# A gram of near tokens held by distance first and group second: one layout changed in a recurrent kernel on one core

## The chip, the cores and the metric

One core of a Trainium2 chip runs the whole program; the other cores are idle. The time is device microseconds from the start to the end of one execution, given as the median of several runs. The profile is that of one execution, and its own time is given beside it. The engines are called as in the profile: PE (TensorE, with PEld for its weight loads), DVE (VectorE), ACT (ScalarE), POOL (GpSimd) and SP (SyncE, which here only issues DMAs).

## What is computed

Two layers. The first is a recurrence over 768 tokens for 4 x 8 heads of 40 channels, in which each head keeps a 40 x 40 state:

```python
for t in range(S):
    y[:, :, t] = np.einsum('bhd,bhde->bhe', rt, state)
    Sa = np.einsum('bhde,bhe->bhd', state, at)
    state_decay = state * wt[:, :, None, :] - np.einsum('bhd,bhe->bhde', Sa, bt)
    state = state_decay + np.einsum('bhd,bhe->bhde', vt, kt)
```

The second takes each token's 320 numbers, normalises them by their root mean square, and puts them through a gated feed-forward layer of 1536 hidden units (`silu(x @ w_gate) * (x @ w_val) @ w_out`).

## The kernel before

The tokens are cut into 24 chunks of 32 (`C`). Inside a chunk the recurrence is replaced by a triangular system of scores between its tokens, so that all heads can be worked on with matmuls. Three functions write the pieces of work of a chunk. `front(c)` (L669) loads w, a, k, b and v, turns them, and makes the scores that only need the inputs; `inverse(c)` (L777), or `early_inverse(c)` (L795) for the first four chunks, inverts the triangle on DVE; `main(c)` (L827) joins it to the state and gives the chunk's outputs. After every second chunk `feed(g)` (L956) puts 64 tokens of each sequence through the feed-forward layer. That layer's matmuls (ps<-xg,wf and po<-wf,sg in the profile, L497) are the largest part of PE's time.

None of this is issued at once. Every operation becomes a `Piece`, and `Plan.issue` (L323) issues the pieces in the order of the list `ORDER` (L33 to L226), written out in the program: which piece comes next on any engine is fixed by that list, not by readiness. PSUM intermediates live in "rooms"; a room takes one of three pairs of PSUM banks, by the list `PAIRS` (L228), so a matmul that fills a pair waits until the last reader of that pair's earlier room is done. Because helpers such as `tt` (L457), `where` (L469), `copy` (L477) and `pe` (L502) record every operation, the profile's lines are those of the helpers: L455 is any DVE operation, L478 any ACT copy, L497 any matmul.

The change lies in `front(c)`, in the scores of near tokens. The 32 tokens of a chunk form 8 groups (g) of 4 tokens (j). Scores inside a group, at distances 1, 2 and 3, are made by one matmul per half and head, with 7 columns per group in the tile `A`: columns 0 to 2 for distance 1, columns 3 and 4 for distance 2 (multiplied by one step of decay), column 6 for distance 3 (by two), and column 5, which stays zero and whose results nobody reads. In order:

- L696: an ACT copy takes the a-part of the turned tile, tokens 1 to 3 of each group, into columns 0 to 2 of `A` (A<-ps in the profile). L697 puts tokens 0 straight into `Ab`, the operand of the next levels.
- L705, L706: two DVE products with the decay `w4` make columns 3 and 4, and column 6 (A<-A,T).
- L708: 32 matmuls per chunk write 56 columns each, 7 for each of 8 groups, into a room (ps<-A,K).
- L711 to L714: three DVE predicated copies, one for each distance, move these scores from PSUM into `LT`, where a mask `near` allows it (LT<-near,ps; they are called the near copies below). In `LT` and in `near` a row has 32 columns, group by group, 4 per group.
- L715 to L722: DVE products and an ACT copy make `K1`, the other operand of the next levels.
- L723 to L725: two DVE products put tokens 1 to 3 of each group into `Ab` (Ab<-A,T).
- L728 to L760: for distances 4, 8 and 16 the same again: a score matmul (ps<-Ab,K, L731), a predicated copy with the mask `msk` (LT<-msk,ps, L733), products and copies for the next level.

`main(c)` later reads scores in a like manner: L887 and L891 multiply them from PSUM by the mask `msi` into `As` (As<-ps,msi), at l=1 every second column, at l=2, 4 and 8 runs of l columns out of every 2l.

Of the kernel before, what the change touches and what calls it, by code (L numbers as in the profile page):

```python
# [9 lines left out]
U32 = mybir.dt.uint32  # L10
# [7 lines left out]
P = 128  # L18
# [361 lines left out]
def kernel(  # L380
# [42 lines left out]
    NI = 2 * N  # L423
# [14 lines left out]
    MUL, ADD, SUB = ALU.mult, ALU.add, ALU.subtract  # L438
    half = lambda i: slice(i * 64, (i + 1) * 64)
    part = lambda i: slice(i * 64, i * 64 + D)  # L440
# [12 lines left out]
    def dve(kind, fn, o, *args):  # L453
        m = lambda at: [at(x) if isinstance(x, bass.AP) else x for x in args]
        plan.add("DVE", kind, lambda at: fn(at(o), *m(at)), [o], aps(*args))  # L455

    def tt(o, a, b, op):  # L457
        dve("tt", nc.vector.tensor_tensor, o, a, b, op)
# [10 lines left out]
    def where(o, m, a):  # L469
        dve("where", nc.vector.copy_predicated, o, m, a)  # L470
# [6 lines left out]
    def copy(o, a):  # L477
        plan.add("ACT", "copy", lambda at: nc.scalar.copy(at(o), at(a)), [o], [a])  # L478
# [17 lines left out]
    def mm(o, lhsT, rhs, start=True, stop=True):  # L496
        return o, lhsT, rhs, lambda at: nc.tensor.matmul(at(o), lhsT, rhs, start=start, stop=stop, skip_group_check=True)  # L497
# [4 lines left out]
    def pe(kind, steps, more=[]):  # L502
        def issue(at):
            return [s[3](at) for s in steps]
        plan.add("PE", kind, issue, [s[0] for s in steps] + more, [x for s in steps for x in s[1:3]])
# [25 lines left out]
    for p0, kt, src in ((0, 0, 0), (0, 1, P), (0, 2, 2 * P), (64, 2, 2 * P)):  # L531
        m = min(P, DM - src)
# [7 lines left out]
    near = const.tile([P, 3, C], FP32, name="near")  # L540
# [39 lines left out]
    whole = lambda t: t  # L580
# [9 lines left out]
    Sd_ = Turns(2, [P, NI * D], "Sd", whole)  # L590
    T_ = Turns(3, [P, NI * 63], "T")
    K_ = Turns(2, [P, NI, 2, C], "K")
    A_ = Turns(1, [P, NI, 8, 7], "A", whole)

    Ab_ = Turns(2, [P, NI, C + D], "Ab")
    for t in Ab_.tiles:
# [38 lines left out]
    each = [(n, i, o) for n in range(N) for i in range(2) for o in range(2)]  # L635
# [33 lines left out]
    def front(c):  # L669
# [5 lines left out]
        for i in range(2):  # L675
# [6 lines left out]
            for x in range(2):  # L682
                at = i * 64 + x * C
# [5 lines left out]
        o = 0  # L689
        for l in LEVELS + (32,):  # L690
            Tl[l] = Tt[:, o:o + NI * C // l].rearrange("p (n t) -> p n t", n=NI)
            o += NI * C // l
        copy(by_i(Tl[1]), ps[:, :, :, 0])
        A, Ab = A_.next(), Ab_.next()
        a4 = ps[:, :, :, 1].rearrange("p n i t -> p (n i) t")
        copy(A[:, :, :, 0:3], a4.rearrange("p n (g j) -> p n g j", j=4)[:, :, :, 1:4])  # L696
        copy(Ab[:, :, 0:C].rearrange("p n (b h j) -> p n b h j", b=2, j=4)[:, :, :, :, 0], a4.rearrange("p n (h b j) -> p n b h j", b=2, j=4)[:, :, :, :, 0])  # L697
        K = K_.next()
        copy(K.rearrange("p (n i) x s -> p n i (x s)", n=N), turned(kb.rearrange("p n o e -> p n (o e)"), slot).rearrange("p n (i s) -> p n i s", i=2))
        LT = z["LT"] = LT_.next()  # L700
        z["KN"] = {1: flat(kb).rearrange("p a e -> p (a e)"), 2: KN_[2].next()}
        tt(z["KN"][2][:, 0:NI * D].rearrange("p (a e) -> p a e", e=D), flat(kb)[:, :, 0:D], wn, MUL)
        w4 = Tl[1].rearrange("p n (g j) -> p n g j", j=4)
        t2 = Tl[2].rearrange("p n (g x) -> p n g x", x=2)
        tt(A[:, :, :, 3:5], A[:, :, :, 1:3], w4[:, :, :, 1:3], MUL)  # L705
        tt(A[:, :, :, 6], A[:, :, :, 4], w4[:, :, :, 1], MUL)  # L706
        gr = plan.room().rearrange("p o (n t) -> p o n t", n=N)
        pe("gramk", [mm(gr[half(i), o, n, 0:56], K[part(o), 2 * n + i].rearrange("p x s -> p (x s)"),  # L708
                        A[part(o), 2 * n + i].rearrange("p g j -> p (g j)")) for n, i, o in each])
        g4 = gr.rearrange("p o n t -> p (o n) t")[:, :, 0:56].rearrange("p n (g j) -> p n g j", j=7)  # L710
        for dist, at in ((1, 0), (2, 3), (3, 6)):  # L711
            m = 4 - dist
            where(LT.rearrange("p n (g j) -> p n g j", j=4)[:, :, :, dist:], near[:, dist - 1:dist].rearrange(
                "p u (g j) -> p u g j", j=4)[:, :, :, dist:].bitcast(U32).to_broadcast((P, NI, 8, m)), g4[:, :, :, at:at + m])  # L714
        K1 = K_.next()  # L715
        lr = lambda t: t.rearrange("p n x (g h) -> p n x h g", h=2)
        tt(lr(K1)[:, :, :, 0], lr(K)[:, :, :, 0], lr(Tl[1][:, :, None])[:, :, :, 1].to_broadcast((P, NI, 2, 16)), MUL)
# [3 lines left out]
            k4 = K1[:, :, x].rearrange("p n (g j) -> p n g j", j=4)[:, :, :, 0:2]  # L721
            tt(k4, k4, t2[:, :, :, 1, None].to_broadcast((P, NI, 8, 2)), MUL)  # L722
        for x in range(2):  # L723
            tt(Ab[:, :, 16 * x:16 * x + 16].rearrange("p n (h j) -> p n h j", j=4)[:, :, :, 1:4], A[:, :, x::2, 0::3],
               w4[:, :, x::2, 0:1].to_broadcast((P, NI, 4, 3)), MUL)  # L725
        tt(Tl[4], t2[:, :, :, 0], t2[:, :, :, 1], MUL)
        K, A = K1, Ab
        for j, l in list(enumerate(LEVELS))[2:]:  # L728
            G = C // (2 * l)
            gr = plan.room().rearrange("p o (n t) -> p o n t", n=N)  # L730
# [7 lines left out]
            t = Tl[l].rearrange("p n (g x) -> p n g x", x=2)  # L738
# [21 lines left out]
            K, A = K1, A1  # L760
# [263 lines left out]
    for c in range(-2, NCH):  # L1024
        if c >= 0:
            main(c)
            if c % CG == CG - 1:
                feed(c // CG)
        if c + 2 < NCH:
            front(c + 2)  # L1030
            (early_inverse if c + 2 < EARLY else inverse)(c + 2)
# [34 lines left out]
```

## Time and profile before

| | |
|---|---|
| median of 3 runs | 1084.85 us (1081.85 to 1085.8) |
| the profiled execution, its own time | 1087.1 us |
| span of its profile, first to last instruction | 1085.0 us |
| mean granted TensorE clock in it | 0.979 |
| HBM traffic over the span | 111 GB/s |

A row of a group gives an operation with its output and inputs, their partitions x elements and how often it ran, then its total busy time, the mean duration in ns of one, the idle time of its engine just before it and what ended that idle time. A row of a timeline gives the start in us from the span's start, the time it took, and the instruction; in brackets stands how long the engine had idled and what released it. [...]

### The profile page before, as it was taken

To read this page: it belongs to the slowest core of one execution; us is meant where nothing else is said; L and a number is where in the kernel's file an instruction comes from. 1 tells how busy PE (TensorE), PEld (TensorE's weight loads), DVE (VectorE), ACT (ScalarE), POOL (GpSimd) and SP (SyncE) were. 2 spreads that over 40 slices of the span, in tenths; PEclk is the share of its full clock that TensorE was granted. 3 is DMA by queue.
4 is the path that set the end of the run, shared out by engine and by line. 5 is a ranking of instruction groups with operands and counts; after the bars stand their busy time and mean duration, and the time that the engine had idled before them with its cause. 6 is when DMAs were issued, how large, how long until landed. Compare 5 with 4: busy or idle time off the path is not lost. (4 is left out here: it accounts for less than half of the span.)

```text
span 1085.0 us, 53343 instructions
## 1 busy us (share of the span) xinstructions
PE 1008.5 (93%) x23406; PEld 828.7 (76%) x23406; DVE 833.1 (77%) x2860; ACT 461.7 (43%) x1043; POOL 309.0 (28%) x553
## 2 busy tenths in 40 slices
PE   7767899899999999999999999999889999999998
PEld 6656777777888787788788788787777787887776
DVE  7977778866868788798798798898778788796420
ACT  6845756643543334334344344434344244342211
POOL 9714404030532131341431321431332331200000
PEclk9978999999999899999999999999999999999999
DMA  9865338785363353555544534553544543623132
GB/s 177 191 164 120 67 93 214 227 166 137 86 139 84 81 130 72 120 107 101 116 92 108 120 92 107 121 111 92 114 89 95 128 109 59 143 70 89 58 103 67
DMA packets 166696, 123.67 MB, mean 114 GB/s; under 512 B 124864, under 2 KB 143232, under 8 KB 166464
## 3 DMA queue, kind: packets, MB, share of 16 engines
q1 hardware_dynamic: 148096, 97.30, 36.6%
q0 software_dynamic: 16192, 22.64, 12.0%
q8 instruction: 184, 3.01, 1.2%
q10 hardware_dynamic: 2176, 0.33, 0.3%
q14 instruction: 48, 0.39, 0.1%
HBM read 104.20 MB, written 15.99 MB: 111 GB/s over the span
## 5 line engine op out<-in xcount | busy, mean ns | idle before, releaser
L497 PE MATMUL ps<-xg,wf 128*128 128x256 f32 (+1 forms) x1728 | 353.9, 392 | 5.0 <-DVE tmp L455 1.4
L497 PEld LDWEIGHTS ps<-xg,wf 128*128 128x128 f32 (+1 forms) x1728 | 261.3, 189 | 60.5 <-issue 16.2
L497 PE MATMUL po<-wf,sg 128*128 128x320 f32 x576 | 181.7, 448 | 0.1
L455 DVE TENSOR_TENSOR tmp<-Yi,M 128x60 f32<-128x60 f32 (+24 forms) x620 | 129.4, 209 | 21.5 <-DMA M<-sB 8.8
L455 DVE TENSOR_TENSOR Yi<-Yi,tmp 128x60 f32<-128x60 f32 (+24 forms) x620 | 130.1, 210 | 12.4
L475 ACT ACTIVATE sg<-ps 128x256 f32<-128x256 f32 x144 | 52.2, 384 | 192.4 <-PE ps L497 192.2
L497 PEld LDWEIGHTS po<-wf,sg 128*128 128x128 f32 x576 | 103.7, 193 | 34.9 <-issue 3.1
L494 POOL DMA_DIRECT2D VU<-in_v_dram x92 | 53.7, 587 | 236.5 <-PE ps L497 154.2
L455 DVE TENSOR_TENSOR sg<-ps,sg 128x256 f32<-128x256 f32 x144 | 58.8, 419 | 59.0 <-ACT sg L475 52.5
L455 DVE TENSOR_TENSOR K<-K,T 128x512 f32<-128x512 f32 (+1 forms) x192 | 93.5, 496 | 8.4 <-PE ps L497 4.1
L497 PEld LDWEIGHTS ps<-Ab,K 40*64 40x64 f32 x4608 | 77.1, 137 | 29.2 <-issue 10.5
L478 ACT COPY KN<-ps 128x640 f32<-128x640 f32 x96 | 66.1, 690 | 75.7 <-PE ps L500 25.5
L497 PE MATMUL ps<-Ab,K 40*64 40x56 f32 x4608 | 86.5, 224 | 11.6 <-ACT K L478 4.7
L494 POOL DMA_DIRECT2D kbn<-in_b_dram x92 | 53.7, 587 | 142.6 <-PE ps L497 141.7
L455 DVE TENSOR_TENSOR As<-ps,msi 128x256 f32<-128x256 f32 (+1 forms) x186 | 79.2, 475 | 16.5 <-PE ps L497 15.4
L478 ACT COPY K<-K 128x256 f32<-128x256 f32 (+1 forms) x168 | 71.8, 443 | 39.1 <-DVE K L455 15.8
L497 PEld LDWEIGHTS ps<-As,KN 128*40 128x40 f32 x3072 | 65.5, 124 | 15.4 <-issue 10.0
L494 POOL DMA_DIRECT2D wn<-in_w_dram x92 | 51.7, 566 | 86.5 <-DVE KN L455 39.2
L497 PE MATMUL ps<-As,KN 128*40 128x32 f32 x3072 | 72.2, 204 | 3.9 <-issue 3.3
L494 POOL DMA_DIRECT2D kbn<-in_k_dram x92 | 53.6, 586 | 74.1 <-PE ps L497 73.3
L455 DVE TENSOR_TENSOR y<-y,ps 128x256 f32<-128x256 f32 x119 | 50.0, 420 | 18.5 <-PE ps L497 16.0
L455 DVE COPY_PREDICATED LT<-near,ps 128x384 f32<-128x384 uint32 (+2 forms) x72 | 52.3, 726 | 5.0 <-PE ps L497 3.9
(130 smaller groups left out, 1542.5 us busy)
## 6 DMA issues: line engine op xcount, KB each, us to landing
wf<-sW SPq DMA_DIRECT2D x104, 480.0 KB, 4.7
M<-sB SPq DMA_DIRECT2D x80, 128.0 KB, 3.3
sW<-ex SPq DMA_DIRECT2D x24, 240.0 KB, 4.4
rn<-in_r_dram SPq DMA_DIRECT2D x24, 160.0 KB, 4.3
out_dram<-ex SPq DMA_DIRECT2D x48, 80.0 KB, 3.2
kbn<-in_k_dram POOLq DMA_DIRECT2D x92, 40.0 KB, 3.3
kbn<-in_b_dram POOLq DMA_DIRECT2D x92, 40.0 KB, 3.6
wan<-in_a_dram POOLq DMA_DIRECT2D x46, 80.0 KB, 5.2
```

The lines of the kernel that those rows point to most:

```text
L455: plan.add("DVE", kind, lambda at: fn(at(o), *m(at)), [o], aps(*args))
L475: plan.add("ACT", "act", lambda at: nc.scalar.activation(at(o), at(a), f, **kw), [o] + aps(acc), [a])
L478: plan.add("ACT", "copy", lambda at: nc.scalar.copy(at(o), at(a)), [o], [a])
L494: plan.add(by, "dma", lambda at: queue.dma_start(out=o, in_=i), [o], [i])
L497: return o, lhsT, rhs, lambda at: nc.tensor.matmul(at(o), lhsT, rhs, start=start, stop=stop, skip_group_check=True)
```

## The change

`A` was held as 8 groups of 7 columns; it becomes 7 columns of 8 groups each. So the seven kinds of column come first and, within one kind, the eight groups lie side by side. The matmul at L708 still takes all 56 columns, and its 56 result columns in PSUM come in the new order. Each operation that writes or reads `A`, or reads those results, keeps its elements and walks them by column kind first and group second: the ACT copy at L696, the products at L705 and L706, the three near copies (whose walk through `LT` and `near` changes with it), and the two products into `Ab` at L723. Layouts of `LT`, `near`, `Ab` and `T` are as before, and so are the order of all instructions, their number, the PSUM pairs and all DMAs.

```diff
-    A_ = Turns(1, [P, NI, 8, 7], "A", whole)
+    A_ = Turns(1, [P, NI, 7, 8], "A", whole)
...
-        copy(A[:, :, :, 0:3], a4.rearrange("p n (g j) -> p n g j", j=4)[:, :, :, 1:4])
+        copy(A[:, :, 0:3], a4.rearrange("p n (g j) -> p n j g", j=4)[:, :, 1:4])
...
-        w4 = Tl[1].rearrange("p n (g j) -> p n g j", j=4)
         t2 = Tl[2].rearrange("p n (g x) -> p n g x", x=2)
-        tt(A[:, :, :, 3:5], A[:, :, :, 1:3], w4[:, :, :, 1:3], MUL)
-        tt(A[:, :, :, 6], A[:, :, :, 4], w4[:, :, :, 1], MUL)
+        w_j = Tl[1].rearrange("p n (g j) -> p n j g", j=4)
+        tt(A[:, :, 3:5], A[:, :, 1:3], w_j[:, :, 1:3], MUL)
+        tt(A[:, :, 6], A[:, :, 4], w_j[:, :, 1], MUL)
         gr = plan.room().rearrange("p o (n t) -> p o n t", n=N)
         pe("gramk", [mm(gr[half(i), o, n, 0:56], K[part(o), 2 * n + i].rearrange("p x s -> p (x s)"),
-                        A[part(o), 2 * n + i].rearrange("p g j -> p (g j)")) for n, i, o in each])
-        g4 = gr.rearrange("p o n t -> p (o n) t")[:, :, 0:56].rearrange("p n (g j) -> p n g j", j=7)
+                        A[part(o), 2 * n + i].rearrange("p j g -> p (j g)")) for n, i, o in each])
+        g4 = gr.rearrange("p o n t -> p (o n) t")[:, :, 0:56].rearrange("p n (j g) -> p n j g", g=8)
         for dist, at in ((1, 0), (2, 3), (3, 6)):
             m = 4 - dist
-            where(LT.rearrange("p n (g j) -> p n g j", j=4)[:, :, :, dist:], near[:, dist - 1:dist].rearrange(
-                "p u (g j) -> p u g j", j=4)[:, :, :, dist:].bitcast(U32).to_broadcast((P, NI, 8, m)), g4[:, :, :, at:at + m])
+            where(LT.rearrange("p n (g j) -> p n j g", j=4)[:, :, dist:], near[:, dist - 1:dist].rearrange(
+                "p u (g j) -> p u j g", j=4)[:, :, dist:].bitcast(U32).to_broadcast((P, NI, m, 8)), g4[:, :, at:at + m])
...
         for x in range(2):
-            tt(Ab[:, :, 16 * x:16 * x + 16].rearrange("p n (h j) -> p n h j", j=4)[:, :, :, 1:4], A[:, :, x::2, 0::3],
-               w4[:, :, x::2, 0:1].to_broadcast((P, NI, 4, 3)), MUL)
+            tt(Ab[:, :, 16 * x:16 * x + 16].rearrange("p n (h j) -> p n j h", j=4)[:, :, 1:4], A[:, :, 0::3, x::2],
+               w_j[:, :, 0:1, x::2].to_broadcast((P, NI, 3, 4)), MUL)
```

## The prediction

> **What bounds the kernel now.** First the page, for the span and the load of each engine, then its chain of work that ended last.
>
> ```profile
> span 1085.0 us, 53343 instructions
> PE 1008.5 (93%) x23406; PEld 828.7 (76%) x23406; DVE 833.1 (77%) x2860; ACT 461.7 (43%) x1043; POOL 309.0 (28%) x553
> PE 16%; issue 4%; DVE 3%; DMA 2%; POOL 1%; ACT 1%; SPq 0%; POOLq 0%; DVEq 0%; ACTq 0%
> ```
>
> TensorE (PE) is busy for 93% of the span and leads the chain, so PE sets the time; every engine's order is written out by hand and stays. The change alters no matmul: the one that makes the near scores still has 56 columns, only named in another order. It alters VectorE (DVE) and ScalarE (ACT) instructions, and it costs or gains only what they make PE wait. Next I read the groups by line with the shapes kept apart, for the instructions that are rewritten and for plain neighbours to measure them against (busy us, mean ns of one, idle before).
>
> ```profile
> L455 DVE TENSOR_TENSOR As<-ps,msi 128x256 f32<-128x256 f32 x144 | 54.2, 415 | 14.0 <-PE ps L497 12.9 <-ACT As L481 0.8
> L455 DVE COPY_PREDICATED LT<-msk,ps 128x256 f32<-128x256 uint32 x72 | 31.2, 433 | 15.3 <-PE ps L497 8.2 <-ACT KN L478 6.3
> L455 DVE TENSOR_TENSOR As<-ps,msi 128x512 f32<-128x512 f32 x42 | 28.4, 680 | 2.5 <-PE ps L497 2.5
> L455 DVE TENSOR_TENSOR Ab<-A,T 128x192 f32<-128x192 f32 x48 | 21.0, 444 | 0.2
> L455 DVE COPY_PREDICATED LT<-near,ps 128x128 f32<-128x128 uint32 x24 | 17.5, 728 | 0.4
> L455 DVE COPY_PREDICATED LT<-near,ps 128x256 f32<-128x256 uint32 x24 | 17.4, 725 | 0.3
> L455 DVE COPY_PREDICATED LT<-near,ps 128x384 f32<-128x384 uint32 x24 | 17.4, 724 | 4.3 <-PE ps L497 3.9 <-DMA LT<-sY 0.2
> L455 DVE TENSOR_TENSOR A<-A,T 128x256 f32<-128x256 f32 x24 | 10.9, 456 | 4.4 <-ACT T L478 3.3 <-ACT A L478 1.0
> L455 DVE TENSOR_TENSOR T<-T 128x256 f32<-128x256 f32 x24 | 10.1, 420 | 2.7 <-ACT T L478 2.5
> L455 DVE TENSOR_TENSOR A<-A,T 128x128 f32<-128x128 f32 x24 | 9.6, 400 | 0.2
> L455 DVE TENSOR_TENSOR T<-T 128x128 f32<-128x128 f32 x24 | 6.9, 286 | 0.1
> L455 DVE TENSOR_TENSOR tmp<-Yi,M 128x70 f32<-128x70 f32 x20 | 4.8, 238 | 0.4
> ```
>
> The two T<-T rows give the plain price: (420 - 286) / 128 = 1.05 ns an element and 420 - 256 * 1.05 = 152 ns fixed. The three predicated copies into LT (the near copies, 24 chunks each) stand far above it, and they take **the same 725 ns for 384, 256 and 128 elements**. What the three share is 128 runs, of 3, 2 and 1 elements: (726 - 152) / 128 = 4.5 ns a run.
>
> **Which side of the copy costs this.** This decides the sign. A run lies in PSUM 7 columns (28 bytes) from the next, in LT and in the mask 4 words (16 bytes). Three rows speak for LT and the mask.
> First, PSUM jumps are cheap elsewhere: among the 415 ns multiplies from sc are those with l=2 (pairs, a jump of 4 columns after each, 128 of them), and those with l=1 read every second column within the 680 ns row; both are at the plain price (152 + 512 * 1.05 = 690).
> Second, the msk copies write 64 pieces of 16 bytes whatever l is. At 4.5 ns a piece that is 152 + 288 = 440, at the plain price 421; they show 433, while multiplies with the same PSUM reads show 415.
> Third, the timeline of one chunk:
>
> ```profile
> 827.42 0.73 DVE L455 COPY_PREDICATED LT<-near,ps 128x384 f32<-128x384 uint32 x1
> 828.02 0.40 DVE L455 TENSOR_TENSOR K<-K,T 128x256 f32<-128x256 f32 x1
> 828.34 0.72 DVE L455 COPY_PREDICATED LT<-near,ps 128x256 f32<-128x256 uint32 x1
> ...
> 828.69 1.24 PE L497 MATMUL po<-wf,sg 128*128 128x320 f32 x4
> ...
> 829.24 0.71 DVE L455 COPY_PREDICATED LT<-near,ps 128x128 f32<-128x128 uint32 x1
> 829.58 0.43 DVE L455 TENSOR_TENSOR tmp<-Yi,M 128x70 f32<-128x70 f32 x1
> ...
> 830.00 1.16 PE L497 MATMUL ps<-Ab,K 40*64 40x56 f32 x64
> ```
>
> The copy of 128 elements lets the next instruction begin after 0.34 us, and that one takes 0.43 us in place of 0.24 (its row above): the reads were done early and results queued up. I read this as a slow write; a slow PSUM read with many requests in flight would look alike, so it is no proof.
> [...]
>
> **The change part by part** (per chunk; 24 chunks).
> *Near copies.* The element order becomes distance, then group, so each element lies 16 bytes from the one before in LT and in the mask, and PSUM is read in runs of 8. The copy at distance 3 has the same LT and mask walk as before; at 728 ns for 128 single visits it is the nearest row for the others. I take its 4.5 ns for each element: 384 give 152 + 384 * 4.5 = 1880, 256 give 1304, 128 stay at 728; together 3912 against 724 + 725 + 728 = 2177, **+1.73 us**. Lower end: the plain price, 555 + 421 + 286 = 1262, -0.92 us.
> *Products into A and Ab on DVE.* The nearest row for words read one by one is the 400 ns product (steps of 28, 28 and 16 bytes): (400 - 152) / 128 = 1.94 ns an element. The 256-element product keeps a single stepped operand, T: at 1.94 it is 649, at 1.05 421 (456 now); the 128-element one 286 to 400; the two into Ab write and read T in single words, 524 at 1.94 (444 now), 354 at 1.05. Taking 1.94: 193 + 0 + 2 * 80 = **+0.35 us**; lower end 2 * (354 - 444) + (421 - 456) + (286 - 400) = -0.33.
> *ACT copy into A.* Its writes become contiguous, its PSUM reads single columns.
>
> ```profile
> L478 ACT COPY T<-ps 128x512 f32<-128x512 f32 x24 | 14.2, 591 | 15.1 <-PE ps L500 13.7 <-DVE Yi L455 1.3
> L478 ACT COPY A<-ps 128x384 f32<-128x384 f32 x24 | 13.9, 579 | 3.9 <-PE ps L500 3.9
> L478 ACT COPY Ab<-ps 128x128 f32<-128x128 f32 x24 | 9.5, 397 | 4.2 <-PE ps L500 4.2
> L478 ACT COPY M<-ps 128x128 f32<-128x128 f32 x8 | 2.2, 277 | 5.0 <-PE ps L497 5.0
> ```
>
> Contiguous: (591 - 277) / 384 = 0.82 ns an element, 172 fixed, so 384 give 487 (-0.09 us). If single columns cost what the Ab row shows, (397 - 172) / 128 = 1.76, it is 848 (+0.27). I take nothing: ACT is busy 43% of the span; without that cover it is at most 24 * 0.27 = 6.5 us.
> *Moves.* None: the same instructions in the same order on every queue, no DMA touched, no wait added.
>
> **What reaches PE.** Behind a near copy stand, in DVE's queue, the K products that the next score matmul (ps<-Ab,K) needs, and in most chunks that matmul writes the pair of PSUM banks that the near copies read. So the lag from the end of the third copy to that matmul is the room for delay. Above it is 830.00 - 829.95 = 0.05 us. Some others:
>
> ```profile
> 370.53 0.72 DVE L455 COPY_PREDICATED LT<-near,ps 128x128 f32<-128x128 uint32 x1
> ...
> 373.82 1.16 PE L497 MATMUL ps<-Ab,K 40*64 40x56 f32 x64
> ...
> 656.60 0.73 DVE L455 COPY_PREDICATED LT<-near,ps 128x128 f32<-128x128 uint32 x1
> ...
> 657.71 0.51 PE L497 MATMUL ps<-Ab,K 40*64 40x56 f32 x19
> ...
> 786.46 2.25 DVE L455 COPY_PREDICATED LT<-near,ps 128x384 f32<-128x384 uint32 x3 [0.61 <-PE ps L497]
> ...
> 788.77 0.45 PE L497 MATMUL ps<-Ab,K 40*64 40x56 f32 x15 [0.38 <-DVE LT L455]
> ```
>
> At 788.77 PE already waits for the copy. Read so for all 24 chunks: nine lags of 0.05 to 0.38 (sum 1.7), four of 0.7 to 1.1 (sum 3.7), one of 1.5, three of 2 to 2.9, and in seven the matmul starts before the third copy ends. The +0.35 us comes earlier, and DVE can lose it while it waits. In the windows from the first A product to the first near copy:
>
> ```profile
> core 0: us, PE busy (x) PEld busy (x) DVE busy (x) ACT busy (x) POOL busy (x), PEclk, DMA share, GB/s
> ...
> 650.40:654.90 4.50, 4.50 (x87) 3.62 (x84) 4.46 (x12) 1.73 (x3) 3.06 (x6) 1.00 0.80 196
> 814.30:827.40 13.10, 12.05 (x184) 9.78 (x184) 10.65 (x38) 4.49 (x10) 2.89 (x6) 1.00 0.78 156
> ```
>
> The first has no idle time to give, the second 2.4 us. Ten chunks have under 0.3 us, so I carry half: the delay at the lag is 1.73 + 0.17 = 1.9 us. PE then loses 9 * 1.9 - 1.7 = 15.4, 4 * 1.9 - 3.7 = 3.9, 0.4, and nothing in three chunks; for the seven I take half the delay, 6.7, between nothing and 13.3 there. **Sum 26.4 us.** It holds if PE's order cannot make up what it loses, which 93% busy suggests. The profiled execution took 1087.1 us (span 1085.0), 0.2% above the median of 1084.85, so 1113 in a profile and **1111 us** beside that median. Ends: everything through, 24 * (1.73 + 0.35) = 50 us, 1135; and below, the rivals.
>
> **Rivals.**
> *A, PSUM's spread columns are the cost (ends on the other side).* Place: the read of ps in the near copies; it decides if the distance-3 copy, whose LT and mask walk is untouched, falls below 700 ns. For it: all three copies jump 28 bytes, which no other DVE row does. Against it: the l=2 multiplies. Then the copies fall to the plain price, -0.92, with +0.35 for the products -0.57 us a chunk; the same share as above (26.4 of 50, half) gives -7 us, 1078; without the product cost -12, 1073. [...]
> *B, single words cost what a plain product pays.* At 1.94 ns the copies take 897 + 649 + 400 = 1946, -0.23, the products +0.35: +0.12 us a chunk, 1.5 us in all, 1086. For it: the 400 ns row, with no queue behind it. Against it: the distance-3 copy at 4.5. [...]
> *C, the slow copies are covered.* DVE idles 1085 - 833 = 252 us; if only the chunks with no lag pass half of it on, 9 * 0.9 = 8 us, 1093. Against it: the wait at 788.77.
>
> **How the numbers follow.** Forecast 0.62; A 0.14; B 0.17; C 0.07. Half a per cent, 5.4 us, is what a measurement here can tell from no change, so same means 1079.4 to 1090.3. A gives faster 0.14; B splits, 0.11 same and 0.06 slower; with the forecast and C slower is 0.75. The range leaves A out and reaches from B to the upper end with a little room: 1084 to 1138.
>
> **What would show it.** [...] The products into A and Ab at about 650, 400 and 524. More waits of PE for LT, and ps<-Ab,K right behind the third copy in most chunks. I am wrong if the copies are slow and the span is not, or if the span grows with the copies at their old price.

## The result and the profile after

The changed kernel took **1127.16 us** (median of 6 runs, 1123.27 to 1136.88), the kernel before 1083.12 us in the same comparison (6 runs, 1075.49 to 1085.8): a ratio of **1.0424, 95% interval 1.037 to 1.0479**, some 46 us slower. The forecast was 1111 us. The profiled execution of the changed kernel took 1123.27 us itself, its span 36.2 us more than that of before. The spans differ by less than the medians because the profiled execution of before (1087.1 us) lies 4.0 us above its median and that of the changed kernel 3.9 us below.

The page of the changed kernel, in the lines that answer to those of before; PEclk is the granted TensorE clock in tenths over 40 equal slices.

```profile
span 1121.2 us, 53343 instructions
PE 1030.3 (92%) x23406; PEld 844.4 (75%) x23406; DVE 879.1 (78%) x2860; ACT 460.6 (41%) x1043; POOL 310.3 (28%) x553
PEclk8776899999999999999999899999999999999999
PE 15%; DVE 5%; issue 4%; DMA 2%; POOL 1%; ACT 1%; POOLq 0%; DVEq 0%; ACTq 0%
```

DVE is busy for 46.0 us more, and its share of the chain goes from 3% to 5%. But PE too is busy for 21.8 us more (1030.3 against 1008.5) with the same 23406 matmuls. The mean granted clock is 0.956, against 0.979; by slices it was, before:

```profile
PEclk9978999999999899999999999999999999999999
```

PE's idle time (span less busy) grows by only 14.4 us, from 76.5 to 90.9.

The groups of the changed kernel by line, shapes apart:

```profile
L455 DVE COPY_PREDICATED LT<-near,ps 128x384 f32<-128x384 uint32 x24 | 44.8, 1868 | 3.3 <-PE ps L497 3.2
L455 DVE COPY_PREDICATED LT<-near,ps 128x256 f32<-128x256 uint32 x24 | 30.9, 1288 | 0.3
L455 DVE TENSOR_TENSOR Ab<-A,T 128x192 f32<-128x192 f32 x48 | 24.6, 521 | 0.2
L455 DVE COPY_PREDICATED LT<-near,ps 128x128 f32<-128x128 uint32 x24 | 17.4, 724 | 0.4
L455 DVE TENSOR_TENSOR A<-A,T 128x256 f32<-128x256 f32 x24 | 14.9, 622 | 2.5 <-ACT T L478 2.5
L478 ACT COPY A<-ps 128x384 f32<-128x384 f32 x24 | 12.1, 503 | 3.1 <-PE ps L500 3.1
L455 DVE TENSOR_TENSOR A<-A,T 128x128 f32<-128x128 f32 x24 | 9.4, 391 | 0.2
L497 PE MATMUL ps<-Ab,K 40*64 40x56 f32 x4608 | 88.3, 228 | 28.9 <-DVE K L455 7.5 <-DVE LT L455 6.2 <-ACT K L478 5.7
```

The near copies take 1868, 1288 and 724 ns. That is 152 + 4.5 ns for each element, as forecast, and 1.70 us more a chunk. The products take 622, 391 and twice 521 ns, 0.31 us more; the ACT copy takes 503 ns, 76 less than before.

The last row holds 28.9 us of idle time ahead of the score matmul; the same row of before, which follows, held 11.6.

```profile
L497 PE MATMUL ps<-Ab,K 40*64 40x56 f32 x4608 | 86.5, 224 | 11.6 <-ACT K L478 4.7 <-issue 3.5 <-ACT ex L475 0.9
```

**Where PE waits.** Two places of the prediction, found again in the timeline of the changed kernel: the copies that began at 786.46 (PE idle 0.38 us at 788.77), and those that began at 827.42 (PE did not wait at 830.00).

```profile
814.85 3.95 DVE L455 COPY_PREDICATED LT<-near,ps 128x384 f32<-128x384 uint32 x3 [0.61 <-PE ps L497]
...
818.85 1.16 PE L497 MATMUL ps<-Ab,K 40*64 40x56 f32 x64 [2.08 <-DVE LT L455]
...
856.31 1.89 DVE L455 COPY_PREDICATED LT<-near,ps 128x384 f32<-128x384 uint32 x1
858.37 1.28 DVE L455 COPY_PREDICATED LT<-near,ps 128x256 f32<-128x256 uint32 x1
859.83 0.70 DVE L455 COPY_PREDICATED LT<-near,ps 128x128 f32<-128x128 uint32 x1
860.58 1.15 PE L497 MATMUL ps<-Ab,K 40*64 40x56 f32 x64 [1.76 <-DVE tmp L455]
```

In the first chunk the three copies take 3.95 us in place of 2.25, and PE's idle time goes from 0.38 to 2.08: 1.70 us longer on DVE, 1.70 us lost on PE. In the second PE waits 1.76 us where it did not wait. The releaser named there is tmp, the DVE instruction issued behind the third copy; the matmul still starts 0.05 us after that copy ends, as before.

Not every wait stands at that matmul. At 303.93 in the changed kernel the wait comes ahead of a matmul in between, at a place where before had none:

```profile
299.91 3.96 DVE L455 COPY_PREDICATED LT<-near,ps 128x384 f32<-128x384 uint32 x3
...
303.93 0.84 PE L497 MATMUL ps<-VU,KN 64*40 64x40 f32 x63 [1.32 <-DVE LT L455]
```

So I measure the stretch from the start of a chunk's first near copy to its score matmul. Summed over the 24 chunks it grows from 76.8 to 102.9 us (+26.1), and PE's idle time inside it from 2.5 to 29.9 us (**+27.4**). The forecast had 26.4 there.

**Two terms that the sum did not have.** The span is 36.2 us longer. The waits behind the near copies are 27.4 of it; PE's idle time everywhere else is 13.0 us less (14.4 - 27.4); and PE's own busy time is 21.8 us more. The last goes with the granted clock. In the records it is either full or half (1.00 or 0.50 of full speed). By the mean clocks, PE had half the clock for (1 - 0.979) * 2 * 1085.0 = 46 us before and (1 - 0.956) * 2 * 1121.2 = 99 us after; 53 us more at half clock and 21.8 us more busy is 0.41 us for each. The two spans, cut at the same point of the work (where chunk 5's near copies begin), first before, then after:

```profile
core 0: us, PE busy (x) PEld busy (x) DVE busy (x) ACT busy (x) POOL busy (x), PEclk, DMA share, GB/s
0.00:190.20 190.20, 151.35 (x4118) 132.10 (x4119) 150.75 (x467) 118.90 (x251) 87.88 (x176) 0.92 0.68 147
190.20:1085.00 894.80, 857.16 (x19290) 696.58 (x19289) 682.34 (x2394) 342.79 (x792) 221.16 (x377) 0.99 0.46 107
```

```profile
0.00:198.40 198.40, 163.90 (x4116) 143.49 (x4117) 160.06 (x468) 119.83 (x252) 88.83 (x176) 0.83 0.66 142
198.40:1121.20 922.80, 866.43 (x19292) 700.94 (x19291) 719.07 (x2394) 340.80 (x792) 221.51 (x377) 0.98 0.45 103
```

In the first fifth, where PE already had the most gaps, the clock falls from 0.92 to 0.83, and PE is busy 12.5 us longer for the same matmuls; its idle time even shrinks, from 38.9 to 34.5. So busier PE is more than the whole loss of 8.2 us there, although PE waits 4.7 us more in the stretches above: its other idle time fell by 9.0. Behind it the 28.0 us are 9.3 of busier PE and 18.7 of idle time.

**What halves the clock.** One and the same wait, in chunk 8, is in the changed kernel and in an experiment below (e2, in which only the copies changed). The timeline of the changed kernel, then of the experiment:

```profile
339.52 1.34 PE L497 MATMUL ps<-Ab,K 40*64 40x56 f32 x64 [1.72 <-DVE K L455]
340.80 3.43 PE L497 MATMUL ps<-xg,wf 128*128 128x256 f32 x8
```

```profile
337.37 1.16 PE L497 MATMUL ps<-Ab,K 40*64 40x56 f32 x64 [1.71 <-DVE K L455]
338.45 1.99 PE L497 MATMUL ps<-xg,wf 128*128 128x256 f32 x8
```

After equal waits, the same eight matmuls take 3.43 us in the one and 1.99 us in the other. In both traces every change of the clock lies on a grid of 3.41 us. Cut on that grid, the same two places read (changed kernel first; the number after POOL's is the clock):

```profile
333.49:336.90 3.41, 3.41 (x18) 2.74 (x18) 3.32 (x6) 1.01 (x1) 0.00 (x0) 1.00 0.69 107
336.90:340.32 3.42, 1.70 (x60) 1.25 (x62) 2.96 (x9) 1.70 (x5) 0.00 (x0) 1.00 0.33 126
340.32:343.73 3.41, 3.41 (x33) 2.77 (x24) 2.61 (x11) 0.41 (x1) 0.00 (x0) 0.50 0.00 0
```

```profile
333.33:336.74 3.41, 2.33 (x14) 1.45 (x12) 2.94 (x7) 1.88 (x4) 0.00 (x0) 1.00 0.90 212
336.74:340.15 3.41, 2.78 (x72) 2.49 (x73) 3.31 (x13) 1.15 (x3) 0.00 (x0) 1.00 0.04 16
340.15:343.56 3.41, 3.41 (x135) 2.70 (x134) 2.23 (x7) 1.64 (x5) 0.00 (x0) 1.00 0.02 5
```

In the changed kernel the wait falls whole into one window: PE is busy for 1.70 of 3.42 us in it, and the next window has half the clock. In the experiment the same wait lies across the border of two windows, PE is busy for 2.33 and 2.78 us in them, and the clock stays full. Counted on this grid over the 13 traces of this case, without the start and the end of each (up to the first fall of the clock, and the window before the last), of the windows with full clock all 47 with PE busy for under 40% were followed by half clock, 26 of 36 with 40 to 50%, 42 of 79 with 50 to 60%, 25 of 133 with 60 to 70%, and 4 of 3527 with 70% or more. So a wait of 1.7 us costs PE itself, or itself and, in these rows, (3.43 - 1.99) + (1.34 - 1.16) = 1.6 us more, by where it lies on the grid.

### The profile page after: what moved, and what is told of

Its sections match the earlier page's. It is cut to its first block, busy times and chain, and to the rows that moved or that the text cites. A ratio compares the mean times of both kernels' runs of the same rounds, so it can differ in the third digit from the quotient of the medians.

```text
span 1121.2 us, 53343 instructions
## 1 busy us (share of the span) xinstructions
PE 1030.3 (92%) x23406; PEld 844.4 (75%) x23406; DVE 879.1 (78%) x2860; ACT 460.6 (41%) x1043; POOL 310.3 (28%) x553
## 5 line engine op out<-in xcount | busy, mean ns | idle before, releaser
L497 PE MATMUL ps<-xg,wf 128*128 128x256 f32 (+1 forms) x1728 | 363.4, 398 | 7.3 <-DVE sg L455 2.6
L497 PEld LDWEIGHTS ps<-xg,wf 128*128 128x128 f32 (+1 forms) x1728 | 267.7, 193 | 65.5 <-issue 16.6
L497 PE MATMUL po<-wf,sg 128*128 128x320 f32 x576 | 182.8, 450 | 0.9 <-DVE sg L455 0.9
L497 PEld LDWEIGHTS po<-wf,sg 128*128 128x128 f32 x576 | 104.3, 194 | 36.2 <-issue 3.7
L497 PEld LDWEIGHTS ps<-Ab,K 40*64 40x64 f32 x4608 | 79.2, 141 | 47.6 <-issue 15.4
L497 PE MATMUL ps<-Ab,K 40*64 40x56 f32 x4608 | 88.3, 228 | 28.9 <-DVE K L455 7.5
L455 DVE COPY_PREDICATED LT<-near,ps 128x384 f32<-128x384 uint32 (+2 forms) x72 | 93.1, 1293 | 3.9 <-PE ps L497 3.2
L497 PEld LDWEIGHTS ps<-As,KN 128*40 128x40 f32 x3072 | 66.3, 125 | 12.3 <-issue 7.2
L497 PE MATMUL ps<-As,KN 128*40 128x32 f32 x3072 | 72.2, 206 | 1.5 <-issue 1.0
L455 DVE TENSOR_TENSOR y<-y,ps 128x256 f32<-128x256 f32 x119 | 50.0, 420 | 14.3 <-PE ps L497 11.6
```

## The experiments

Ratios are to the kernel before, run on the same chip. A time without an interval is one execution; the kernel before, beside those, took 1095.59 us, which lies above all its other runs, so that only durations are read from them.

**Which part costs: the copies or the rest.** e1_groups_first keeps the new layout and all else, but the near copies walk group by group again, through `LT`, `near` and `g4` as in the lines removed by the change:

```diff
-        g4 = ....rearrange("p n (j g) -> p n j g", g=8)
+        g4 = ....rearrange("p n (j g) -> p n g j", g=8)
...
-            where(LT.rearrange("p n (g j) -> p n j g", j=4)[:, :, dist:], near...
+            where(LT.rearrange("p n (g j) -> p n g j", j=4)[:, :, :, dist:], near...
```

> The changed kernel, with the three near copies alone walking group first again: LT and the mask in runs of 3, 2 and 1 as before the change, PSUM in single columns 8 apart. Price per 16-byte piece of LT and mask (theory L): the copies are back at 725 ns each, whatever PSUM's order. If PSUM's order has a price of its own (rival P): the copies of 384 and 256 elements take over 800. The products into A and Ab stay at 622, 391 and 521, the ACT copy at 503, so DVE has about 24 * 0.31 = 7.5 us more than before the change. Time: if nearly all DVE delay reaches PE (theory T) +6 us on the kernel before, about 1089; if half reaches it and the rest of the loss came from the granted clock (rival C) +4, about 1087.

Measured: 1075.61 us against 1077.14, ratio 0.9996, 0.9965 to 1.0027; neither of the two expected losses, 4 and 6 us, came. The groups of this kernel:

```profile
L455 DVE COPY_PREDICATED LT<-near,ps 128x128 f32<-128x128 uint32 x24 | 17.5, 729 | 0.4
L455 DVE COPY_PREDICATED LT<-near,ps 128x384 f32<-128x384 uint32 x24 | 17.4, 726 | 3.2 <-PE ps L497 3.0
L455 DVE COPY_PREDICATED LT<-near,ps 128x256 f32<-128x256 uint32 x24 | 17.4, 726 | 0.3
```

PSUM is read here in single columns, 8 apart, and the copies still take 726 ns: the order of the PSUM columns costs and gains nothing. Rival A is out. The slower products (624, 394 and 523 ns) are in this kernel as well, and cost nothing that can be measured.

e2_copies_only is its mirror: the old layout, and only the copies walk by distance first.

```diff
-        g4 = ....rearrange("p n (g j) -> p n g j", j=7)
+        g4 = ....rearrange("p n (g j) -> p n j g", j=7)
...
-            where(LT.rearrange("p n (g j) -> p n g j", j=4)[:, :, :, dist:], near...
+            where(LT.rearrange("p n (g j) -> p n j g", j=4)[:, :, dist:], near...
```

> The kernel before, with the three near copies alone walking distance first: A and the products as before, LT and the mask word by word, PSUM in single columns 7 apart. Theory L: 1868, 1288 and 725 ns as in the changed kernel, though PSUM's columns are not neighbours. Rival P: more than that, above 2000 for 384 elements, since PSUM now jumps too. DVE has 24 * 1.71 = 41 us more than before. Time: theory T (0.8 to 0.9 of it reaches the end) +33 to +37, 1116 to 1120; rival C, the forecast's share of one half and little from the rest: +22, 1105, with the granted clock near that of the kernel before.

Measured: 1115.91 us, ratio 1.0382, 1.0329 to 1.0435. The copies take 1866, 1288 and 724 ns. Nearly the whole loss comes with the copies' walk alone, and it is more than either expectation (22, or 33 to 37 us): some 41. Between this kernel and e1, on one chip, the profiled spans differ by 38.9 us: 18.2 of busier PE (1027.2 against 1009.0) and 20.7 of idle time, with clocks of 0.958 and 0.977. In the stretches from the first near copy to the score matmul PE idles 24.3 us more (27.9 against 3.6).

**Which side of the copy.** Three kernels take its operands apart. e3_mask_dense stores the mask in the order in which the copies read it:

```diff
-        ts(near[:, dist], bits, float(dist + 1), None, ALU.is_equal)
-        tt(near[:, dist], near[:, dist], same, MUL)
+        nd = near[:, dist].rearrange("p (j g) -> p g j", g=8)
+        ts(nd, bits.rearrange("p (g j) -> p g j", j=4), float(dist + 1), None, ALU.is_equal)
+        tt(nd, nd, same.rearrange("p (g j) -> p g j", j=4), MUL)
...
-                "p u (g j) -> p u j g", j=4)[:, :, dist:]...
+                "p u (j g) -> p u j g", g=8)[:, :, dist:]...
```

> The changed kernel with the mask near stored in the order in which the copies now walk it, so that it is read from neighbouring words; LT is still written word by word, 16 bytes apart. If the price is that of writing LT (theory LT): 1868, 1288 and 724 ns stay. If it is that of reading the mask: 152 + 1.05 an element, 555, 421 and 286. If both share it: in between, some 1000 to 1400 for 384 elements.

Measured: 1861, 1286 and 723 ns, and 1120.39 us. The mask's order is not it.

e4_target_dense has the copies write neighbouring words:

```diff
-            where(LT.rearrange("p n (g j) -> p n j g", j=4)[:, :, dist:], near...
+            where(LT.rearrange("p n (j g) -> p n j g", g=8)[:, :, dist:], near...
```

> The changed kernel with the near copies writing neighbouring words of LT (at other places than the scores belong to, so the near scores are lost), the mask still read word by word, 16 bytes apart. Theory LT: 555, 421 and 286 ns, or up to 1.94 ns an element, 897, 649 and 400, if reading the mask word by word costs what it costs a plain product. If the price is that of the mask: 1868, 1288 and 724 stay.

Its groups:

```profile
L455 DVE COPY_PREDICATED LT<-near,ps 128x384 f32<-128x384 uint32 x24 | 20.3, 845 | 3.1 <-PE ps L497 2.9
L455 DVE COPY_PREDICATED LT<-near,ps 128x256 f32<-128x256 uint32 x24 | 14.7, 611 | 0.3
L455 DVE COPY_PREDICATED LT<-near,ps 128x128 f32<-128x128 uint32 x24 | 9.2, 382 | 0.3
```

Its near scores stand in wrong places, so that only its durations count. The step of 16 bytes in LT makes the copy dear: without it 845 ns in place of 1868. What is left is (845 - 611) / 128 = 1.83 ns an element, with the mask still read in single words.

e5_multiply_new puts a plain product in the copy's place, score by mask into the same words of LT:

```diff
-            where(LT..., near...bitcast(U32)..., g4...)
+            tt(LT..., g4..., near..., MUL)
```

> The changed kernel with each near copy replaced by a product of the scores and the mask into the same words in the same order (the three overwrite each other, so the scores at distance 1 and 2 are partly lost). If it is the predicate that makes single words dear (theory predicate): 1.94 ns an element as in the 400 ns product before, 897, 649 and 400. If any write of single words 16 bytes apart costs this: 1868, 1288 and 724 stay.

```profile
L455 DVE TENSOR_TENSOR LT<-ps,near 128x384 f32<-128x384 f32 x24 | 20.5, 854 | 3.4 <-PE ps L497 2.6 <-DMA out_dram<-ex 0.7
L455 DVE TENSOR_TENSOR LT<-ps,near 128x256 f32<-128x256 f32 x24 | 14.8, 618 | 0.3
L455 DVE TENSOR_TENSOR LT<-ps,near 128x128 f32<-128x128 f32 x24 | 9.4, 392 | 0.3
```

With the same walk on all sides a product takes 854 ns where the copy takes 1868. So it is not the step in LT alone but **the predicated write in such a step**: 4.5 ns for each 16-byte place visited, against 1.84 ns for a product, (854 - 618) / 128.

e6_multiply_old does the same in the kernel before, in its own walk:

```diff
-            where(LT..., near...bitcast(U32)..., g4...)
+            tt(LT..., g4..., near..., MUL)
```

> The kernel before with each near copy replaced by a product of the scores and the mask, walking group first (the three overwrite each other, so scores are lost as in the run above). Theory predicate: for 384, 256 and 128 elements at least the plain price, 555, 421 and 286, and at most what 128 visits at 1.94 add, 560, 425 and 400. If any write of single words costs 4.5 ns a visit: 725 each.

Measured: 552, 420 and 388 ns where the copies took 724, 725 and 728, and 1073.81 us in one execution, without the scores that the later products overwrite. At 384 elements in runs of 3 the product is at the plain price that the prediction worked out (555); at 128 single words it pays (388 - 152) / 128 = 1.84 ns each.

e7_first_multiply does it for distance 1 alone, in the kernel before:

```diff
-            where(LT..., near..., g4[:, :, :, at:at + m])
+            lt, mask = LT..., near...
+            if dist == 1:
+                tt(lt, g4[:, :, :, at:at + m], mask..., MUL)
+            else:
+                where(lt, mask..., g4[:, :, :, at:at + m])
```

> The kernel before with the near copy at distance 1 alone made a product of scores and mask; it comes first, so what it zeroes is written by the later copies, and the output stays the reference's. Theory predicate: 384 elements in about 555 to 560 ns in place of 724, 24 * 0.165 = 4 us less of DVE, and at the share seen for small delays (one half) 2 us less time: ratio 0.996 to 1.0, within what can be told from no change. If single visits cost this in any write: 725 ns and no difference.

Measured: the first copy falls to 553 ns, and the ratio is 0.9989, 0.9946 to 1.0031. Cutting 0.17 us a chunk brings nothing that can be measured, and so none of the kernels compared over several executions is faster than the one before.

**How the delay becomes time.** Two kernels delay the old one by copies of the old walk: the distance-3 copy is issued twice in e8_third_twice, four times in e11_third_four_times, whose edit this is.

```diff
+    def twice(o, m, a):
+        def fn(*x):
+            return [nc.vector.copy_predicated(*x) for _ in range(4)]
+        dve("where", fn, o, m, a)
...
-            where(LT...
+            (twice if dist == 3 else where)(LT...
```

> The kernel before, with the near copy at distance 3 issued twice in a row (the second writes the same values again): a known delay of DVE and nothing else, 24 * 0.6 to 0.73 = 14 to 17 us of DVE time, at the place in its queue where the change put its delay. Theory T: 0.8 to 0.9 of it reaches the end, +12 to +14, 1095 to 1097. The forecast's share of one half: +8, 1091.

> The kernel before with the near copy at distance 3 issued four times in a row: 3 * 0.6 to 0.73 = 1.8 to 2.2 us of DVE a chunk, about what the change adds, by copies that keep their old walk. If the delay of DVE is all that matters: ratio 1.038 to 1.05, like the near copies walked distance first (1.038), with time at half clock near 100 us and idle PE time before ps<-Ab,K near 24 us. If the walk itself disturbs something else: 1.02 to 1.03 (the forecast's share, 24 to 28 us of the added 43 to 53).

Measured beside the two kernels with the changed walk:

| kernel | DVE busy time added a chunk | ratio, 95% interval | added us | of DVE's added time |
|---|---|---|---|---|
| e8, copy twice | 0.65 us (15.6 in all) | 1.0073, 1.003 to 1.0115 | 7.9 | 0.5 |
| e2, copies' walk | 1.60 us (38.5) | 1.0382, 1.0329 to 1.0435 | 41 | 1.1 |
| changed kernel | 1.92 us (46.0) | 1.0424, 1.037 to 1.0479 | 46 | 1.0 |
| e11, copy four times | 2.05 us (49.2) | 1.0537, 1.0454 to 1.0619 | 58 | 1.2 |

DVE's busy time is that of each page less the 833.1 us of before. The column "added us" is the ratio less 1, times the median of before. The delay alone does it, without any change of a walk or a layout. And it is not proportional: a small delay passes on half of itself, the smaller of e8's two expectations; a large one passes on all of itself or more, e11 a little more than expected (1.0537 for 1.038 to 1.05). In e11 PE is busy 1029.7 us at a clock of 0.956, as in the changed kernel.

**Trying to take the clock's share away.** Both of the next kernels are the changed one with matmuls added that compute nothing, in places where PE waits for the score matmul: eight in each of 21 chunks (e9_warm), or two to six, by chunk, in 11 chunks with long waits (e10_fill). The edit of e9:

```diff
+        self.grams, self.outs = {}, 0
...
+            if p.kind == "gramk":
+                self.grams[p.key[1]] = self.grams.get(p.key[1], 0) + 1
+                if self.grams[p.key[1]] == 2 and (self.outs < 12 or self.outs % 12):
+                    for _ in range(8):
+                        self.warm()
+            self.outs += p.kind == "out"
```

> The changed kernel, with 8 idle matmuls (128x128, into an unused part of the po tile) issued on PE just before the first ps<-Ab,K matmul of a chunk, in the chunks where po is not being read: they fill the time in which PE waits for the near copies. Rival C, the falling granted clock makes much of the loss: time at half clock goes from 100 us back towards 50, mean granted clock to 0.97 or more, and the time falls by 8 to 15 us against the changed kernel, to 1112 to 1119. Theory T, the waits themselves are the loss: the time stays within 4 us of 1127, or rises where a wait was shorter than the 1 us that these matmuls take.

> The changed kernel with idle matmuls (2 to 6 in a chunk, about 0.27 us each) only in the 11 chunks where the changed kernel's PE waits 0.7 to 3.8 us right before ps<-Ab,K, and not more than fit the wait. Rival C (the granted clock, falling after such waits, makes a good part of the loss): time at half clock falls from 100 us to 70 or less, PE's other work is shorter by half of that, and the time falls by 5 to 15 us against the changed kernel: ratio to the kernel before 1.028 to 1.037 in place of 1.042. Theory T (only the waits): ratio 1.042 or more.

Measured: 1157.74 us, ratio 1.0778, 1.0718 to 1.0839, and 1148.78 us, ratio 1.0675, 1.0609 to 1.074. Both lose more than the changed kernel; **neither settles the question**. In e9 eight such matmuls take 2.0 us, not the 1 us expected, and overfill the waits: the time at half clock fell, from 99 to (1 - 0.967) * 2 * 1157.9 = 76 us, and PE's busy time less the added 21 * 2.0 us is some 1018 us against 1030.3, but the span grew by 36.7. e10 has only 41 of them, some 10 us. Its six executions show clocks of 0.946 to 0.960, the changed kernel's 0.951 to 0.961: the clock did not rise, and PE stalled in other places. Its waits at matmuls into `ps` (L497, in e10 L504) that the profile puts down to PE's own issue (us in total, times, longest; the trace is of an execution of 1158.61 us), then those of the changed kernel, then those of before:

```profile
PE ps L504 <- issue: 32.0, 28, 2.4
```

```profile
PE ps L497 <- issue: 12.0, 14, 1.6
```

```profile
PE ps L497 <- issue: 24.5, 28, 2.3
```

e10 has 20 us more of them than the changed kernel, but before, without any added matmul, has 12.5 more as well. What goes with these waits, the DMA records of the traces show. On the pages of before and of the changed kernel stands a queue of its own for instructions (packets, MB, share):

```profile
q8 instruction: 184, 3.01, 1.2%
```

184 transfers for 23406 matmuls are one for every 127.2. Counted along PE's order, 289 of the 293 waits of this kind in the 13 traces stand at the same place of such a block of 127 matmuls, and all 293 end 1.1 to 1.9 us after a transfer of this queue has ended. I read them as PE waiting for its next block of instructions, which no run tests, and call them waits for instructions. Over all its matmuls PE waits so for 26.9 us in before, 13.0 in the changed kernel and 40.9 in e10; why added matmuls make it more, these runs don't show.

## Why the prediction was right, and where it was not

- **PE sets the time, and the change reaches it only through waits**: held. PE stays at 92%, and e11 gets a loss at least as large (1.0537) from delay alone.
- **The near copies at 1880, 1304 and 728 ns, by a price per 16-byte place visited on the LT side**: 1868, 1288 and 724. The reading of the three equal 725 ns was right, and e4 and e5 say more: it is the write into LT, not the mask (e3), and only when it is predicated. A plain product in the same walk is charged too, but far less: 1.84 ns a word (e5), against 1.05 at the plain price.
- **Products at 649, 400 and 524 ns**: 622, 391 and 521, so +0.31 us a chunk and not +0.35. I carried half of it as delay; e1 has all of it and shows no loss (0.9996, 0.9965 to 1.0027). That half, 0.17 us a chunk, was too much.
- **ACT copy at no cost, between 487 and 848 ns**: 503, faster by 76 ns. Reading single PSUM columns is cheap there too, which leaves its stepped write as the old copy's slow side.
- **Rival A** (PSUM columns): the distance-3 copy stayed at 724, and e1 rules it out directly. **Rival B** (plain price for single words): its 897, 649 and 400 ns are nearly what a product takes (854, 618 and 392 in e5), but the copy is no product. **Rival C** (covered): PE waited 27.4 us.
- **What reaches PE, by the lags: 26.4 us.** In the stretch that it spoke of, PE lost 27.4. By the prediction's five kinds of chunks, forecast and growth of PE's idle time in the stretch:

| lag in the trace of before | chunks | forecast us | measured us |
|---|---|---|---|
| 0.05 to 0.38 us | 9 | 15.4 | 13.2 |
| 0.7 to 1.1 | 4 | 3.9 | 3.9 |
| 1.5 | 1 | 0.4 | 0.2 |
| 2 to 2.9 | 3 | 0 | 4.2 |
| negative | 7 | 6.7 | 5.9 |

The three long lags were no slack. In chunk 9 (copies to 370.53 in the rows of the prediction) PE had run eight po<-wf,sg matmuls at half clock, 4.26 us in that execution against 2.42 in the trace of after; with full clock the lag is 0.24 us, as e1 shows. In chunk 8 the K products that the matmul needs stand behind the third copy and fill the lag; in chunk 23 a matmul in between waited. So the close sum is in part luck: the 4.2 us of these three chunks stand against 3.2 too much in the others.

- **The step that failed: the sum of 26.4 us taken as the change in time, "if PE's order cannot make up what it loses, which 93% busy suggests".** Two terms were missing, of opposite signs. PE's order did make up some: its idle time outside those stretches fell by 13.0 us, and its waits for instructions alone fell by 13.9 (26.9 to 13.0). They are fewer wherever DVE delays PE much: 11.6 to 13.6 us in the changed kernel, e2, e3 and e11, against 17.6 to 26.9 in before, e1 and e4 to e8. But before has the most of these seven, so the 13.0 belong in part to that one execution; between e1 and e2 only 24.3 - 20.7 = 3.6 us were made up. And the waits lowered PE's granted clock (0.979 to 0.956), which made the same matmuls 21.8 us longer. So 27.4 - 13.0 + 21.8 = 36.2 us between the profiled spans, and some 46 us by the ratio. The rows for it stood on the page of before: a mean clock of 0.979 and idle stretches in which it fell. The prediction counted only how long PE waits, not what a wait of half a window does to the work behind it.
- **How far this is shown.** That equal waits are followed by half clock or not, by their place on the grid, is seen in the traces, as is the doubled time of the matmuls there. That the share of this in the loss is about 20 us is an accounting, and an upper one: +21.8 between the profiled spans, +18.2 between e2 and e1, and over all executions a mean clock of 0.951 to 0.961 in the 6 of the changed kernel against 0.965 to 0.983 in 36 of the kernel before on the study's chips. In those 36 the time falls by 8.5 us for each 0.01 of clock (least squares, correlation -0.75), and 0.023 would be some 20 us; but a wait can also lengthen the time and lower the clock at once. Nor need the two missing terms be independent: in the first fifth, where PE became 12.5 us busier, its waits for instructions fell from 11.8 to 3.9 us, as they would if a slower PE filled idle time that it had; no run isolates that. If all the 13.0 us came so, the clock would cost 36.2 - 27.4 = 8.8 us on balance, if none, 21.8. It was not shown by taking the clock's share away; e9 and e10 failed at that.

The direction, the part that costs and the price per element were right for the reasons given. The total was 16 us short, within the range.

## What to carry to other kernels

Where copies of different sizes take the same time, count the places that they visit on the side they write, and keep neighbouring words together there: for a predicated copy it was worth 1.1 us of 1.9 to write three words in one visit. When DVE feeds a PE that is over 90% busy, price a new wait by the stretch from the slowed instruction to the next matmul that needs it, then ask whether such waits leave PE busy for less than some 60% of a window of 3.41 us, and so cost it its clock as well (in these traces 115 of 162 such windows with full clock were followed by half clock, and 29 of 3660 others); a slack that is read from one execution must be read at full clock.

## What the runs showed of the hardware that was not expected

- A predicated copy that writes one fp32 word every 16 bytes takes 4.5 ns a word (1868 ns for 384, 724 for 128), and as much for a visit of two or three words (726 ns for 128 visits); a product in the same walk takes 1.84 ns a word (854 ns for 384).
- Reading PSUM in single columns 7 or 8 apart costs a predicated copy nothing (726 ns against 724 with columns 8 apart, 1866 against 1868 with 7 apart), and an ACT copy of 384 that reads so and writes contiguously takes 503 ns, against 579 with the sides the other way.
- The granted clock changed only on a grid of 3.41 us: a window with full clock and PE busy for under 40% was always followed by half clock (47 of 47), one with 70% or more hardly ever (4 of 3527), and in between the more often the less PE was busy.
- PE has waits that the profile puts down to its own issue, nearly all at one place in every 127 matmuls (289 of 293) and all of them ending 1.1 to 1.9 us after a transfer of the instruction queue: 26.9 us of the span in the trace of before, 11.6 to 40.9 us over the 13 traces.
- Forty-one added matmuls that compute nothing made the changed kernel some 27 us slower by the ratios (1.0675 against 1.0424), though they take some 10 us; the waits for instructions were 40.9 us in its trace, against 13.0.
